# Six unread products in TensorE's pauses of the first attention batch, and a PSUM bank set aside for them

## The chip, the cores and the metric

The kernel runs on one core of a Trainium2 chip. The metric is the device time of one execution in microseconds (us). The core has TensorE (PE: matrix products, with PEld for its weight loads), VectorE (DVE), ScalarE (ACT), GpSimd (POOL) and SyncE (SP, whose queue issues every DMA here). TensorE's clock is granted by the chip at one of two levels, 2.4 GHz (written 1.00 in the profile) or 1.2 GHz (0.50).

## The reference

Three parts follow one another on 4 batches of 576 positions. First attention with 8 heads of 64: four heads look at the last 32 positions, four at positions of the same residue modulo 32. Then a maxout layer of width 768 and a PReLU layer of width 2048.

```python
scores = scale * np.matmul(q, k.transpose(0, 1, 3, 2))
scores = np.where(masks[None, :, :, :], scores, -1000000000.0)
attn = np.exp(scores - np.max(scores, axis=-1, keepdims=True))
attn = attn / (np.sum(attn, axis=-1, keepdims=True) + 1e-09)
x = np.matmul(attn, v)                                  # then laid out as (2304, 512)
x = np.maximum(np.maximum(x @ w1, x @ w2), x @ w3) @ w_out
h = x @ w_in
out = (np.maximum(h, 0.0) + alpha * np.minimum(h, 0.0)) @ w_out2
```

## The kernel before

The program has two halves. In the first (to about 396 us) attention and the maxout layer of the four batches are woven together; in the second (L959, L802) the PReLU layer runs over three blocks of 768 rows. The change touches the first half alone.

The weaving is done by the class `Weave`. Each piece of work is a task with an engine, a cost, a position and what it needs and gives. `plan` goes through them once, on the host, with these planned costs (in ns): it keeps the time at which each engine is free, picks the next task that can start, and writes down an order. `run` then emits every task in that order, so that the order on each engine is fixed in the program. Buffers are counted as rings: `place` lets a task that makes a buffer start only when the user of the buffer made so many places earlier is done. PSUM is one such ring, of eight banks of 512 columns, and nearly every task of PE takes one.

A unit of attention (`attention_tasks`) is two heads of one group of positions; a batch has eight units. On PE it runs `scores` (L314, a product in float32 of 64 rows, of which the trace shows two instructions), two `transposes` (L355) and `values` (L380). Between them stand DVE's masking with the row minimum (L322), ACT's exponential (L329), DVE's reciprocal (L340, L341), the normalising by DVE (L262) or ACT (L260), a copy of the transposes (L247, name pt) and the split of the result into a high and a low part (L247 and L250, name x). PE's order puts scores of one unit between transposes and values of others.

The products of the maxout layer (`gate_products`, L542, and `out1_products`, L564) are float32r products of 288 columns, twelve or eighteen to a task. Their weights come through SP's queue as words of a double (L425), are joined by ACT and DVE (L439, L443, L445) and split by ACT and DVE into a high and a low part (L247, L250, name w). From about 42 us on these products fill PE.

The constants (the identity and three masks) are made by POOL in `build_constants`, before everything else.

Of the kernel before, what the change touches and what calls it, by code (L numbers as in the profile page):

```python
# [10 lines left out]
F32 = mybir.dt.float32  # L11
# [7 lines left out]
DM = 512  # L19
F1 = 768  # L20
F2 = 2048
P = 128
# [6 lines left out]
QT = 96  # L29
KT = 128  # L30
# [14 lines left out]
class Weave:  # L45
# [11 lines left out]
    def __init__(self, rings):  # L57
        self.rings, self.made = dict(rings), {ring: [] for ring in rings}
        self.tasks, self.givers, self.users, self.banks = [], {}, {}, set()
        self.order = {ring: [] for ring in ("q", "v", "e", "pt", "x", "word")}  # L60

    def add(self, engines, emit, pos, needs=(), gives=(), makes=(), uses=(), mode=None, slack=0):
        t = len(self.tasks)
        if engines[0][0] != "PE" and any(key in self.banks for key in uses):
            pos -= self.URGENT
        self.banks.update(key for ring, key in makes if ring == "bank")
        self.tasks.append((engines, emit, pos, needs, makes, mode, slack))
        for ring, key in makes:
            if ring in self.order:
                self.order[ring].append(key)  # L70
        for e in gives:
            self.givers.setdefault(e, []).append(t)
        for key in [key for _, key in makes] + list(uses):
            self.users.setdefault(key, []).append(t)
# [19 lines left out]
    def plan(self, seed=None, near=120, change=100, slack=1.0, delay=350, shift=0.0):  # L94

        rng = random.Random(seed)
        sway = [rng.uniform(-shift, shift) if task[2] > -self.URGENT / 2 else 0.0 for task in self.tasks]
        delays = {"PE": 300, "ACT": delay, "DVE": delay, "SP": 2300}
        self.made = {ring: [] for ring in self.rings}
        free = dict.fromkeys(delays, 0)  # L100
        left = [sum(len(self.givers[e]) for e in task[3]) for task in self.tasks]
        at = [0] * len(self.tasks)
        ready = {t for t, n in enumerate(left) if not n}
        done, mode, order = {}, None, []
        while ready:
            options = {}
            for t in ready:
                engines, _, pos, _, makes, m, wait = self.tasks[t]
                when = self.place(makes, done)
                if when is None:  # L110
                    continue
                when = max(when, at[t] + slack * wait)
                best = None
                for e, cost in engines:
                    start = max(when, free[e])
                    if best is None or start + cost < best[0] + best[2]:
                        best = (start, e, cost)
                start, e, cost = best
                if m is not None:
                    start += change * (m != mode)  # L120
                options.setdefault(e, []).append(
                    (start, pos + sway[t] - (m is not None and m == mode), t, cost))
            pick = None
            for e, c in options.items():
                first = min(o[0] for o in c)
                o = min((o for o in c if o[0] <= first + near), key=lambda o: (o[1], o[0], o[2]))
                if pick is None or o[0] < pick[1][0]:
                    pick = (e, o)
            e, (start, _, t, cost) = pick
            makes, m = self.tasks[t][4:6]  # L130
            ready.remove(t)
            order.append((t, e))
            for ring, key in makes:
                self.made[ring].append(key)
            mode = mode if m is None else m
            free[e] = start + cost
            done[t] = start + cost + delays[e]
            for u in self.takers.get(t, ()):
                left[u] -= 1
                same = e == "PE" == self.tasks[u][0][0][0]  # L140
                at[u] = max(at[u], start + cost if same else done[t])
                if not left[u]:
                    ready.add(u)
        assert len(done) == len(self.tasks)
        return order

    def run(self, **settings):
        self.takers = {}
        for t, task in enumerate(self.tasks):
            for e in task[3]:  # L150
                for g in self.givers[e]:
                    self.takers.setdefault(g, []).append(t)
        for t, e in self.plan(**settings):
            self.tasks[t][1](e)


@with_exitstack
def attention_maxout_prelu_kernel(
# [13 lines left out]
    nc = tc.nc  # L172
    PSUM = bass.MemoryType.PSUM
    ctx.enter_context(tc.manual_schedule())

    const = ctx.enter_context(tc.tile_pool(name="const", bufs=1, side="left"))
    ident = const.tile([P, P], F32, name="ident")
    mask_l = const.tile([QT, KT], F32, name="mask_l")
    mask_l0 = const.tile([QT, KT], F32, name="mask_l0")
    mask_s = const.tile([P, 126], F32, name="mask_s")  # L180
    alpha_sb = const.tile([P, NF2], F32, name="alpha_sb")

    def build_constants():
        g = nc.gpsimd
        make_identity(nc, ident)
        for m in (mask_l0, mask_l):
            g.memset(m, 0.0)
            g.affine_select(out=m, in_=m, compare_op=ALU.is_ge, fill=BIG, base=32,
                            pattern=[[-1, KT]], channel_multiplier=1)
            g.affine_select(out=m, in_=m, compare_op=ALU.is_ge, fill=BIG, base=-1,  # L190
                            pattern=[[1, KT]], channel_multiplier=-1)
        g.affine_select(out=mask_l0, in_=mask_l0, compare_op=ALU.is_ge, fill=BIG, base=-32,
                        pattern=[[1, KT]], channel_multiplier=0)
        g.memset(mask_s, 0.0)
        ms = mask_s.rearrange("p (r a) -> p r a", a=NA)
        g.affine_select(out=ms, in_=ms, compare_op=ALU.is_ge, fill=BIG, base=0,
                        pattern=[[-NA, 7], [-1, NA]], channel_multiplier=1)
        g.affine_select(out=ms, in_=ms, compare_op=ALU.is_ge, fill=BIG, base=NA - 1,
                        pattern=[[NA, 7], [0, NA]], channel_multiplier=-1)
# [10 lines left out]
    hx, xx, x0x, ax, psx, conv_x = (ExitStack() for _ in range(6))  # L210

    def pool(stack, name, bufs, side="left"):
        return stack.enter_context(tc.tile_pool(name=name, bufs=bufs, side=side, reuse_waits="tile"))
# [19 lines left out]
    raw_p = pool(conv_x, "raw", 3, "right")  # L233
    words_p = pool(conv_x, "words", 8, "right")
    wst = pool(conv_x, "wst", 2, "right")
    ps = psx.enter_context(tc.tile_pool(name="ps", bufs=8, space=PSUM))

    def bank():
        return ps.tile([P, 512], F32, tag="bank", name="bank")


    weave = Weave({"bank": 8, "q": 2, "v": 2, "e": 3, "pt": 4, "x": 11, "t": 4, "h": 12,
                   "raw": 3, "word": 8, "wst": 2})
    add, tl = weave.add, {}

    def copy(e, out_, in_):
        (nc.scalar.copy if e == "ACT" else nc.vector.tensor_copy)(out_, in_)  # L247
# [478 lines left out]

    homes = [("gate", f, g) for f in range(NF1) for g in range(3)] + [("mix", f) for f in range(NF1)]
    build_constants()
    nc.sync.dma_start(alpha_sb, alpha)
    for b in range(B):  # L730
# [282 lines left out]
    for n in range(NQ * NBLK):  # L1013
        blk, q = divmod(n, NQ)
# [73 lines left out]
```

## Time and profile before

| | |
|---|---|
| median of 3 runs | 763.51 us (762.62 to 764.78) |
| profiled execution | 764.85 us, of which the span of instructions is 762.9 us |
| PE busy | 741.8 us, 97% of the span |
| DVE, ACT busy | 596.8 and 454.7 us (78% and 60%) |
| mean granted clock of TensorE | 0.991 |

The profile is one execution. Its span runs from the first to the last instruction; the 1.95 us between it and the execution's own time lie around it. A busy share is a mean over stages that differ much, so the stretches are looked at one by one.

### The profile page before, as it was taken

The numbers are of one execution on the slowest core, as the hardware profiler recorded it, in microseconds if no ns is written. First come the engines' busy times: TensorE is split into PE (matmuls) and PEld (weight loads), VectorE is DVE, ScalarE is ACT, GpSimd is POOL, SyncE is SP. The second block draws the span as 40 slices with busy tenths as digits, with TensorE's granted clock in tenths as the row PEclk, the third lists the DMA queues.
The fourth block names the chain that finished last, engine by engine and source line by source line (L and its number), as shares of the span: only waits on it lengthen the run. The fifth ranks groups of instructions, "written<-read, shape, count | busy, mean of one in ns | idle before, by whom it ended". The sixth has DMA issues, their size and how long they took to land.

```text
span 762.9 us, 16093 instructions
## 1 busy us (share of the span) xinstructions
PE 741.8 (97%) x5704; PEld 723.0 (95%) x5704; DVE 596.8 (78%) x1670; ACT 454.7 (60%) x1226; POOL 3.2 (0%) x16
## 2 busy tenths in 40 slices
PE   5899999999999999999999999999999999999997
PEld 4699999999999999999999999999999999999997
DVE  5999999888777987336368988878888877888894
ACT  6988897756665775323246566624666644566561
POOL 1000000000000000000000000000000000000000
PEclk9699999999999999999999999999999999999999
DMA  7387769877878856566938889999888999878361
GB/s 245 130 259 232 240 216 326 271 273 255 300 248 282 270 202 213 171 259 192 362 113 285 273 289 320 386 403 334 291 285 301 354 401 328 273 239 259 121 194 59
DMA packets 85471, 199.37 MB, mean 261 GB/s; under 512 B 10640, under 2 KB 40848, under 8 KB 85392
## 3 DMA queue, kind: packets, MB, share of 16 engines
q1 hardware_dynamic: 85392, 198.35, 75.9%
q8 instruction: 45, 0.74, 0.4%
q14 instruction: 34, 0.28, 0.1%
HBM read 148.51 MB, written 49.81 MB: 260 GB/s over the span
## 4 chain that ended last, share of the span: by engine, by line
PE 77%; DVE 12%; DMA 5%; ACT 2%; issue 2%; SPq 1%; DVEq 0%; ACTq 0%
PE bank L542 27%; PE ph L959 20%; PE po L802 15%; PE bank L564 9%; PE bank L314 3%; PE bank L380 2%; PE bank L355 2%; DVE g L796 2%; DVE c L806 2%; DMA w<-wh 1%; DMA w<-wp 1%; DVE e L322 1%; DMA xs<-x 1%; DMA x<-xd 1%; DVE c L964 1%
## 5 line engine op out<-in xcount | busy, mean ns | idle before, releaser
L542 PE MATMUL bank<-x,w 128*128 128x288 f32 x1728 | 236.5, 297 | 0.3 <-DVE t L553 0.3
L542 PEld LDWEIGHTS bank<-x,w 128*128 128x128 f32 x1728 | 231.1, 189 | 2.1 <-DVE t L553 0.6
L959 PE MATMUL ph<-x,w 128*128 128x384 f32 x1008 | 203.4, 337 | 1.8 <-DVE c L964 1.2
L802 PE MATMUL po<-w,g 128*128 128x256 f32 x1296 | 183.8, 282 | 1.7 <-DVE g L796 0.8
L802 PEld LDWEIGHTS po<-w,g 128*128 128x128 f32 x1296 | 175.4, 189 | 4.2 <-DVE g L796 3.2
L959 PEld LDWEIGHTS ph<-x,w 128*128 128x128 f32 x1008 | 168.3, 188 | 3.0 <-DVE c L964 1.9
L964 DVE TENSOR_TENSOR c<-ph,c 128x384 f32<-128x384 f32 x168 | 91.0, 554 | 32.7 <-PE ph L959 31.8
L795 ACT CAST g<-c 128x384 fp32r<-128x384 f32 x96 | 48.5, 505 | 89.7 <-DVE c L946 53.0
L564 PE MATMUL bank<-h,w 128*128 128x288 f32 x576 | 79.9, 297 | 0.4 <-DVE nm L322 0.4
L564 PEld LDWEIGHTS bank<-h,w 128*128 128x128 f32 x576 | 76.9, 188 | 1.8 <-DVE nm L322 0.8
L250 DVE TENSOR_TENSOR w<-word,w 128x512 fp32r<-128x512 f32 x88 | 55.4, 637 | 23.9 <-ACT w L247 23.5
L329 ACT ACTIVATE e<-e,nm 96x128 f32<-96x128 f32 (+2 forms) x176 | 68.0, 394 | 6.0 <-DVE nm L322 6.0
L916 ACT ACTIVATE c<-c 128x384 f32<-128x384 f32 x96 | 50.5, 526 | 33.9 <-DVE c L964 32.9
L247 ACT CAST w<-word 128x512 fp32r<-128x512 f32 x88 | 50.6, 582 | 32.0 <-DMA wh<-w 17.7
L917 ACT ACTIVATE c<-c,nalpha 128x384 f32<-128x384 f32 x96 | 59.2, 617 | 3.1
L920 DVE SCALAR_TENSOR_TENSOR c<-c 128x384 f32<-128x384 f32 x96 | 53.0, 552 | 9.0 <-ACT c L917 9.0
L796 DVE TENSOR_TENSOR g<-c,g 128x384 fp32r<-128x384 f32 x96 | 52.9, 551 | 1.9 <-ACT g L795 1.9
L796 DVE TENSOR_TENSOR g<-k,g 128x384 fp32r<-128x384 f32 x72 | 36.8, 550 | 14.4 <-ACT g L795 14.4
L439 ACT ACTIVATE word<-raw 128x512 f32<-128x512 f32 x56 | 37.4, 677 | 11.5 <-DMA raw<-in_w 5.9
L445 DVE SCALAR_TENSOR_TENSOR word<-raw,word 128x512 uint32<-128x512 uint32 x56 | 38.8, 693 | 1.9
L631 DVE TENSOR_TENSOR t<-bank,t 128x288 f32<-128x288 f32 x72 | 32.6, 452 | 7.8 <-PE bank L542 7.1
L795 ACT CAST g<-k 128x384 fp32r<-128x384 f32 x72 | 33.4, 515 | 7.8 <-PE po L802 4.4
(72 smaller groups left out, 679.8 us busy)
## 6 DMA issues: line engine op xcount, KB each, us to landing
w<-wh SPq DMA_DIRECT2D x72, 512.0 KB, 5.0
raw<-in_w SPq DMA_DIRECT2D x50, 512.0 KB, 4.5
w<-wo SPq DMA_DIRECT2D x48, 512.0 KB, 5.9
w<-wp SPq DMA_DIRECT2D x36, 512.0 KB, 6.3
wh<-w SPq DMA_DIRECT2D x24, 512.0 KB, 3.7
xd<-xst SPq DMA_DIRECT2D x28, 384.0 KB, 3.5
x<-xd SPq DMA_DIRECT2D x28, 384.0 KB, 8.1
wp<-w SPq DMA_DIRECT2D x24, 256.0 KB, 3.0
```

What stands on the lines that cost most here:

```text
L247: (nc.scalar.copy if e == "ACT" else nc.vector.tensor_copy)(out_, in_)
L250: nc.vector.tensor_tensor(out=out_, in0=x, in1=y, op=ALU.subtract)
L329: nc.scalar.activation(tl[ek][:nq, j, i, :nk], tl[ek][:nq, j, i, :nk], AF.Exp, bias=tl["nm", u][:nq, j, i:i + 1], scale=-1.0, accum_out=tl ...
L542: nc.tensor.matmul(acc, words["gate", f, g][:, wi, cc * P:(cc + 1) * P], xt[b, cc, hf][:, xi, :], start=n == 0, stop=n == 3 * NCC - 1)
L564: nc.tensor.matmul(acc, words["mix", f][:, wi, dc * P:(dc + 1) * P], st["h", hf, f][:, xi, :], start=n == 0, stop=n == 3 * NF1 - 1)
L795: nc.scalar.copy(g[:, 0], x)
L796: return g, lambda: nc.vector.tensor_tensor(out=g[:, 1], in0=x, in1=g[:, 0].bitcast(F32), op=ALU.subtract)
L802: nc.tensor.matmul(bank[:, NH * half:NH * (half + 1)], g[:, gi, t * P:(t + 1) * P], w[:, wi, off:off + NH], start=first and i == 0, stop=l ...
L917: nc.scalar.activation(a, a, AF.Copy, scale=nalpha[:, f:f + 1])
L920: nc.vector.scalar_tensor_tensor(out=a, in0=h, scalar=0.0, in1=a, op0=ALU.max, op1=ALU.add)
L959: nc.tensor.matmul(bank, words["h", n, i][:, wi, off + c * P:off + (c + 1) * P], x2h[blk, k, c][:, xi, :], start=m == 0, stop=m == 5)
L964: nc.vector.tensor_tensor(out=out_, in0=bank, in1=other, op=ALU.add)
```

## The change

Six products whose result nobody reads are put on PE in the first batch. Their operand is a tile `dense` of 96 x 128 float32 numbers, made by an `iota` on POOL ahead of the other constants (into the place of `mask_l0`, as integers) and a converting copy on DVE. One product has `dense` as its weights and the same tile, repeated four times, as its 512 moving columns. It writes a PSUM bank of its own, which is taken from the ring of the other tasks: that has seven banks now.

Where the planner finds a task of PE that starts more than 900 planned ns after PE is free (but not counting what lies before 1500 ns, and not from 46000 ns on), it puts products ahead of that task in the order: two ahead of PE's first task, and for every later pause its length over 1700, rounded down. They are not counted in the planner's own times.

```diff
@@ class Weave
+    FILL_FIRST, FILL_FROM, FILL_UNTIL, FILL_LEAST, FILL_COST = 2, 1500, 46000, 900, 850
@@ plan
             ready.remove(t)
+            idle = start - max(free[e], self.FILL_FROM)
+            if e == "PE" and start < self.FILL_UNTIL and idle > self.FILL_LEAST:
+                n = int(idle // (2 * self.FILL_COST)) if free[e] else self.FILL_FIRST
+                order.append((None, n))
             order.append((t, e))
@@ run
         for t, e in self.plan(**settings):
-            self.tasks[t][1](e)
+            if t is None:
+                self.fill(e)
+            else:
+                self.tasks[t][1](e)
@@ attention_maxout_prelu_kernel
+    dense = const.tile([QT, KT], F32, name="dense")
     def build_constants():
         g = nc.gpsimd
+        numbers = mask_l0.bitcast(mybir.dt.int32)
+        g.iota(numbers, pattern=[[7919, KT]], base=1234567, channel_multiplier=104729)
+        nc.vector.tensor_copy(dense, numbers)
         make_identity(nc, ident)
...
-    ps = psx.enter_context(tc.tile_pool(name="ps", bufs=8, space=PSUM))
+    ps = psx.enter_context(tc.tile_pool(name="ps", bufs=7, space=PSUM))
+    idle_ps = psx.enter_context(tc.tile_pool(name="idle_ps", bufs=1, space=PSUM))
...
-    weave = Weave({"bank": 8, "q": 2, "v": 2, "e": 3, "pt": 4, "x": 11, "t": 4, "h": 12,
+    weave = Weave({"bank": 7, "q": 2, "v": 2, "e": 3, "pt": 4, "x": 11, "t": 4, "h": 12,
                    "raw": 3, "word": 8, "wst": 2})
+    idle_bank = idle_ps.tile([P, 512], F32, name="idle_bank")
+    wide = dense[:, None, :].to_broadcast([QT, DM // P, P])
+    def fill(n):
+        for _ in range(n):
+            nc.tensor.matmul(idle_bank[:, :DM], dense, wide, start=True, stop=True)
+    weave.fill = fill
```

## Rows read from the trace of the kernel before

**Rows 1.** The page: engines' busy time, PE's clock in 40 slices, shares of the chain.

```profile
PE 741.8 (97%) x5704; PEld 723.0 (95%) x5704; DVE 596.8 (78%) x1670; ACT 454.7 (60%) x1226; POOL 3.2 (0%) x16
...
PEclk9699999999999999999999999999999999999999
...
PE 77%; DVE 12%; DMA 5%; ACT 2%; issue 2%; SPq 1%; DVEq 0%; ACTq 0%
```

**Rows 2.** Windows: stretch, its length, busy of PE, PEld, DVE, ACT, POOL, PEclk, DMA.

```profile
5.00:16.00 11.00, 7.93 (x60) 6.61 (x62) 7.57 (x59) 7.99 (x39) 0.00 (x0) 1.00 0.93 299
16.00:26.20 10.20, 6.77 (x84) 4.94 (x81) 8.78 (x61) 10.01 (x46) 0.00 (x0) 1.00 0.45 145
26.20:40.00 13.80, 12.73 (x89) 10.65 (x90) 12.01 (x57) 11.33 (x45) 0.00 (x0) 0.51 0.44 142
42.40:130.00 87.60, 87.11 (x749) 84.31 (x748) 85.15 (x283) 73.89 (x234) 0.00 (x0) 1.00 0.77 252
```

**Rows 3.** Waits of PE after 42.3 us: total, times, longest, the largest group.

```profile
PE ph L959 <- DVE c L964: 1.2, 3, 0.5
```

**Rows 4.** Groups by form, PE, 5 to 14 us: scores of the 108 form.

```profile
L314 PE MATMUL bank<-k,q 64*108 64x108 f32 x24 | 2.8, 403 | 6.1 <-DMA k<-in_kTs 6.1
```

**Rows 5.** The same view, 27 to 34 us.

```profile
L314 PE MATMUL bank<-k,q 64*108 64x108 f32 x12 | 1.4, 406 | 0.0
```

**Rows 6.** The same view, 40 to 42.3 us.

```profile
L314 PE MATMUL bank<-k,q 64*108 64x108 f32 x12 | 0.7, 254 | 0.0
```

**Rows 7.** Timeline of PE, 4 to 22 us: start, length, work, idle before.

```profile
5.02 2.30 PE L314 MATMUL bank<-k,q 64*108 64x108 f32 x20 [5.02 <-DMA k<-in_kTs]
8.37 1.42 PE L314 MATMUL bank<-k,q 64*108 64x108 f32 x12 [1.05 <-DMA k<-in_kTs]
11.79 1.30 PE L355 MATMUL bank<-ident,e 108*108 108x108 f32 x6 [2.00 <-DVE e L262]
...
19.65 0.67 PE L355 MATMUL bank<-ident,e 108*108 108x108 f32 x3 [1.48 <-DVE e L262]
20.25 0.90 PE L314 MATMUL bank<-k,q 64*96 64x128 f32 x12
```

**Rows 8.** Timeline of PE, 22 to 60 us.

```profile
26.47 0.72 PE L355 MATMUL bank<-ident,e 96*128 96x96 f32 x3 [2.22 <-DVE e L262]
...
34.34 1.49 PE L355 MATMUL bank<-ident,e 96*128 96x96 f32 x6 [0.80 <-ACT e L260]
35.53 3.23 PE L542 MATMUL bank<-x,w 128*128 128x288 f32 x12
...
39.85 0.72 PE L355 MATMUL bank<-ident,e 96*128 96x96 f32 x6
...
42.35 17.86 PE L542 MATMUL bank<-x,w 128*128 128x288 f32 x133
```

**Rows 9.** Waits of ACT, 6 to 43 us: total, times, longest.

```profile
ACT pt L247 <- PE bank L355: 1.7, 3, 0.7
ACT x L247 <- PE bank L380: 1.7, 4, 0.8
```

**Rows 10.** Waits of DVE, 6 to 43 us.

```profile
DVE e L322 <- PE bank L314: 9.9, 6, 6.6
DVE x L250 <- ACT x L247: 1.5, 3, 0.8
DVE pt L247 <- PE bank L355: 0.5, 1, 0.5
```

**Rows 11.** Timeline of all engines, 0 to 30 us: POOL's constants, DVE's first work.

```profile
0.74 0.20 POOL masks.py:197 MEMSET ident<- 128x128 f32 x1 [0.29 <-POOLq L1079]
...
3.92 0.33 POOL L198 TENSOR_SCALAR_AFFINE_SELECT mask_s<-mask_s 128x126 f32<-128x126 f32 x1
...
6.56 0.27 DVE L322 CUSTOM_DVE_ANT_0 e<-bank,mask_s 108x108 f32<-108x108 f32 x1 [6.56 <-PE bank L314]
```

**Rows 12.** Timeline of DVE, 26 to 50 us: the third weight's low part.

```profile
43.22 0.69 DVE L250 TENSOR_TENSOR w<-word,w 128x512 fp32r<-128x512 f32 x1
```

More of the change, by code (lines that the diff above doesn't have):

```diff
@@ L60, in __init__, with fill @@
         self.order = {ring: [] for ring in ("q", "v", "e", "pt", "x", "word")}
+    FILL_FIRST, FILL_FROM, FILL_UNTIL, FILL_LEAST, FILL_COST = 2, 1500, 46000, 900, 850
+    def fill(self, n):
+        raise NotImplementedError
     def add(self, engines, emit, pos, needs=(), gives=(), makes=(), uses=(), mode=None, slack=0):
```

## The prediction

> **What bounds the kernel now.** The page comes first: PE is busy 97% of the span and carries 77% of the chain that ended last; its clock stands at a full digit except in the second of 40 slices [rows 1]. The windows then show where that share holds. From 42.4 us PE is busy 87.11 of 87.60 us, while between 5 and 40 us it is not [rows 2], and after 42.3 us its largest group of waits is 1.2 us [rows 3]. So from 42 us on PE sets the pace, and what the start gains or loses is carried to the end, as long as DVE, at 85.15 of 87.60 us almost as full, comes forward with it.
>
> Next, the clock. The windows give 0.51 from 26.2 to 40 us and 1.00 before [rows 2]. The second figure can't be taken as read. The same scores (64x108) take 403 ns in the mean before 14 us [rows 4], 406 ns in the stretch marked 0.50 [rows 5], and 254 ns after 40 us [rows 6]. Until some time before 16 us TensorE therefore ran at 1.2 GHz too; the profile has no record of the clock there. In the timeline it is at 2.4 GHz by 20.25 us (twelve scores of 128 columns in 0.90 us) [rows 7], and low again from the transposes at 26.47 us, behind a pause of 2.22 us, through the first maxout products (twelve in 3.23 us, against 133 in 17.86 us from 42.35 us on, which is 1.61 for twelve) [rows 8].
>
> Last, whom the slow clock holds up. Between 6 and 43 us ACT waits for PE 1.7 and 1.7 us [rows 9], DVE 9.9 us of which 6.6 us is the start, then 1.5 us behind ACT and 0.5 us [rows 10]: 3.4 us of ACT, 5.3 of DVE. In between, from 16 to 26.2 us at the full clock, ACT is busy 10.01 of 10.20 us [rows 2]: there ACT sets the pace, not PE.
>
> **Where the six products go.** The planner's own starts (its planned ns, not times of the chip), followed through the tasks of before, have PE idle 2676 ahead of the first scores, 1574 ahead of the third scores, and 3015, 2160, 2190 and 1910 ahead of four transposes; all others up to 46000 are under 900. By the rule that is two, none, and four times one: six. The four places are those where the trace has PE waiting 2.00, 1.48, 2.22 and 0.80 us [rows 7, 8].
>
> **Price of one.** The trace has no such product. Of a float32 product it shows two instructions, so 1024 columns. Twelve scores of 128 columns in 0.90 us make 0.59 ns a column [rows 7], which gives 0.60 us; these use half the rows each and may overlap. Six transposes of 96 in 0.72 us make 1.25 ns [rows 8], which gives 1.28 us. I take 0.85 us, near the middle and what the diff counts with; at the low clock 1.7 us, between 1.2 and 2.56 us.
>
> **The two at the start.** POOL's first constant starts at 0.74 us; an iota between a memset (0.20) and a select (0.33), then a DVE copy like its 0.27 us row [rows 11], and the hand-overs, make `dense` ready at about 1.5 us (an estimate). Two at the low clock end at 1.5 + 3.4 = 4.9 us, just before the scores' operands at 5.02 us [rows 7]; by the bounds between 3.9 and 6.6, so 0 to 1.6 us late. I take 0. POOL's other constants move back by that third of a us, and the memset of `mask_l0` waits for DVE's copy; behind it in POOL's queue stand the masks, the last done at 3.92 + 0.33 = 4.25 us and first read at 6.56 [rows 11]. That cover is 2.3 us; without it every unit would start late by what is over. DVE has nothing before 6.56. No DMA is added or moved, and SP's queue stays as it is.
>
> **The four in pauses.** At the full clock 0.85 us fits into 2.00, 1.48 and 2.22 us, and is 0.05 us over in 0.80 us [rows 7, 8]: nothing, at most 0.48 us by the upper price.
>
> **What they may bring.** With PE at 2.4 GHz from the first scores to 42 us, PE alone would need about half of 7.93 and of 12.73 us [rows 2] less: 10 us. This is no forecast, since others hold the pace then. The third weight shows it: its low part is done at 43.22 + 0.69 = 43.91 us [rows 12], and its unit, the second after 42.35 [rows 8], starts at 42.35 + 1.61 = 43.96. PE can't come forward further than DVE and ACT do. ACT's idle time in 26.2 to 40 us is 13.80 - 11.33 = 2.47 us [rows 2], all inside the slow stretch; PE's work there shrinks by some 6 us, so I take 2.4 us as gone. Of ACT's 3.4 us of waits [rows 9] 0.9 us are left for the start; ACT can't begin earlier than its first scores, and when the clock rises between 5 and 16 us is open, so I take 0.6. Sum: 2.4 + 0.6 - 0 - 0 = 3.0 us. The far end is DVE's 5.3 us.
>
> **The seventh bank.** In the planner's record of before, three of 284 banks taken by the eighth place were still held by the task seven places back, by 34, 247 and 602 planned ns; the others had been free. So the order should stay nearly the same. Taken: 0; far end 0.9 us, if all three are waits on the chip.
>
> **Does one product hold the clock?** The clock fell behind the pause of 2.22 us, and not behind those of 2.00 and 1.48 us, of which the first is in the low stretch anyway [rows 7, 8]. In the stretch that followed PE was busy 12.73 of 13.80 us, and yet it stayed at 1.2 GHz until about 40 us [rows 2]. So it isn't shown that 0.85 us more in a pause is enough. The Trainium skill (TensorE: Matmul & The Clock Gate, Part 1, "What's actually happening") lets the clock follow how busy PE has recently been, by which any work in the pause would do. Its Part 4 (PE-mode transpose) says that transposes don't count as busy in the same way, which speaks against the change, because three of the four pauses lie between other work and transposes. By the first the sum stands at 3.0 us, by the second the clock may fall beside the products. The trace of the slow stretch leans to the second.
>
> **The rivals.** (1) My forecast: the clock rises with the first scores or soon after, and is held to 42 us. 3.0 us less. (2) It rises early and is not held behind 24 us: the 2.4 us fall away, 0.6 stays, with up to 0.5 more or less: 762.4 to 763.4. For it: the busy stretch that stayed low. (3) The clock is held, but DVE's weights don't come forward, because they wait for loads or for other DVE work: DVE is full from 42 us [rows 2] and the third weight has no slack [rows 12]; 763.0 or so. Against it: DVE has 5.3 us of waits to give before that. (4) Slower: the clock stays low and the products are in the way of PE's next task. At 1.7 us each they are over by 0.22 and 0.90 us: 1.1 us, 764.6. At 2.56 us it is 1.6 + 0.56 + 1.08 + 0.34 + 1.76 = 5.3 us, 768.8. It counts as slower from a price of about 2.0 us on (0.5 + 0.5 + 1.2 = 2.2). Against it: two dense products in a row are more work for PE than anything else before 16 us. (5) The bank ring makes another order or waits: 763.5 to 764.4, more if the order turns out worse all through.
>
> **How the numbers follow.** The sum against the profiled execution is 764.85 - 3.0 = 761.85 us; that execution lies 1.34 us above the median shown, so the forecast is 763.51 - 3.0 = 760.5 us. Faster or slower counts from 0.3% on, 2.3 us, about what a measurement of this kernel can tell from no change. Chances: (1) 0.55, with 758.6 to 761.6 as its own range (0.50 faster, 0.05 same); (2) 0.18 (0.02 faster, 0.16 same); (3) 0.12 same; (4) 0.10 (0.07 slower, 0.03 same); (5) 0.05 (0.03 same, 0.02 slower). Together 0.52 faster, 0.39 same, 0.09 slower. The range goes from DVE's 5.3 us less, 758.2, to rival 4 at its taken price, 764.6.
>
> **What the profile will show.** Right: the 64x108 scores near 254 ns from 8 us on, PEclk 1.00 from 26 to 40 us, the dense run of maxout products starting near 39.4 instead of 42.35 us, and ACT's and DVE's waits for PE before 43 us mostly gone. Six products of two instructions at the named places, each 0.6 to 1.28 us. Wrong: PEclk 0.5 again behind 24 us (2), PE waiting for w or t after 40 us (3), products of 2 us and transposes starting later behind them (4), PE waiting for a bank's reader (5).

## The result: 0.74% slower, where 0.4% faster was forecast

Over 12 runs each the changed kernel takes 771.94 us in the median (766.11 to 774.44), the kernel before 765.54 us (762.62 to 769.39). The ratio is 1.0074, 95% interval 1.0050 to 1.0098, some 5.7 us. The forecast was 760.5 us with a range up to 764.6 us; it took off from the 763.51 us of three runs. The profiled execution of the changed kernel has a span of 772.5 us; at 774.32 us it is one of the slowest of the twelve.

The page of the changed kernel: busy time of the engines, and PE's clock in 40 slices.

```profile
PE 754.3 (98%) x5718; PEld 727.4 (94%) x5718; DVE 600.4 (78%) x1680; ACT 453.0 (59%) x1217; POOL 3.4 (0%) x17
...
PEclk9899999999999999999999999999999999999999
```

PE has 14 instructions more than in [rows 1], so seven products and not six; most of its 12.5 us of longer busy time are these (10.9 us), and they lie in what were pauses. Its windows, in the stretches of [rows 2]:

```profile
5.00:16.00 11.00, 10.40 (x65) 7.33 (x64) 7.76 (x59) 8.28 (x40) 0.00 (x0) 1.00 0.90 306
26.20:40.00 13.80, 12.92 (x115) 10.03 (x115) 12.99 (x67) 12.80 (x55) 0.00 (x0) 0.75 0.37 130
42.40:130.00 87.60, 83.23 (x689) 79.51 (x689) 80.91 (x263) 68.54 (x214) 0.00 (x0) 0.98 0.73 245
```

Behind 26.2 us the clock is at 0.75 in the mean where it was 0.51, and ACT is busy 12.80 us instead of 11.33: that much went as meant. The loss is in the last row. From 42.4 to 130 us PE is busy 83.23 us, not 87.11. The timeline of PE, 0 to 62 us, to be held against [rows 7, 8]:

```profile
1.38 3.78 PE L270 MATMUL idle_bank<-dense 96*128 96x512 f32 x4 [1.38 <-DVE dense L202]
5.12 2.30 PE L342 MATMUL bank<-k,q 64*108 64x108 f32 x20
...
24.64 1.05 PE L270 MATMUL idle_bank<-dense 96*128 96x512 f32 x2
27.08 0.69 PE L383 MATMUL bank<-ident,e 96*128 96x96 f32 x3 [1.39 <-DVE e L290]
...
33.55 1.88 PE L270 MATMUL idle_bank<-dense 96*128 96x512 f32 x2
35.27 0.81 PE L383 MATMUL bank<-ident,e 96*128 96x96 f32 x6
...
40.80 1.12 PE L270 MATMUL idle_bank<-dense 96*128 96x512 f32 x2
41.36 2.54 PE L570 MATMUL bank<-x,w 128*128 128x288 f32 x14
44.46 17.76 PE L570 MATMUL bank<-x,w 128*128 128x288 f32 x132 [0.57 <-DVE w L278]
```

Behind the two products the scores start at 5.12 us, 0.1 us later than before; a product takes 1.8 to 1.9 us at the low clock and, where it stands alone, 1.04 to 1.12 us at the high one. The 20 scores behind them take 2.30 us, as before: the clock did not rise. The groups by form, 5 to 14 us, say the same (403 ns in [rows 4], 254 ns at 2.4 GHz in [rows 6]):

```profile
L342 PE MATMUL bank<-k,q 64*108 64x108 f32 x24 | 2.8, 403 | 0.6 <-DMA k<-in_kTs 0.6
```

By 41.36 us PE is 1.0 us ahead of the kernel before, and a seventh product, which the other order brought, stands in front of that. Then it waits. Waits of PE from 42.3 to 420 us (total, times, longest), where the kernel before has 2.2 us in all, the longest 0.7 us:

```profile
PE bank L383 <- DVE x L278: 1.7, 1, 1.7
PE bank L570 <- DVE x L278: 1.5, 1, 1.5
PE bank L570 <- ACT pt L275: 1.5, 1, 1.5
PE bank L570 <- DVE t L581: 1.0, 1, 1.0
PE bank L383 <- DVE t L659: 0.9, 1, 0.9
PE bank L342 <- ACT pt L275: 0.6, 1, 0.6
PE bank L570 <- DVE w L278: 0.6, 1, 0.6
```

With one more of 0.2 us these are 8.0 us, 5.8 more. Two of the places are followed by a stretch at the low clock (windows behind the waits at 125.7 and at 283.6 us; the last figures are PEclk, DMA share and GB/s):

```profile
127.00:130.50 3.50, 3.50 (x25) 3.22 (x25) 3.36 (x11) 3.15 (x13) 0.00 (x0) 0.54 0.59 228
284.00:287.60 3.60, 3.60 (x19) 3.60 (x18) 3.52 (x10) 2.97 (x13) 0.00 (x0) 0.54 1.03 306
```

In each some 3.4 us run at half speed, which costs about 1.7 us. 5.8 + 3.4 = 9.2 us. To be explained are the difference of the two spans, 772.5 - 762.9 = 9.6 us, and the 1.0 us by which PE led at 41.36 us, so some 1.4 us stay open. In this execution the loss lies behind 42 us, in PE waiting for readers of its banks and in the falls of the clock behind two such waits, and not in the products. How much of the 5.7 us between the kernels such falls make isn't shown: over the twelve runs the mean granted clock is 0.994, no lower than over the 35 runs of the kernel before that were made beside e1.

### The profile page after: what moved, and what is told of

The parts are those of the page before. It is cut to its first block, busy times and chain, and to the rows that moved or that the text cites. A ratio compares the mean times of both kernels' runs of the same rounds, so it can differ in the third digit from the quotient of the medians.

```text
span 772.5 us, 16118 instructions
## 1 busy us (share of the span) xinstructions
PE 754.3 (98%) x5718; PEld 727.4 (94%) x5718; DVE 600.4 (78%) x1680; ACT 453.0 (59%) x1217; POOL 3.4 (0%) x17
## 4 chain that ended last, share of the span: by engine, by line
PE 68%; DVE 15%; DMA 9%; ACT 4%; issue 3%; SPq 1%; DVEq 0%; ACTq 0%
PE ph L987 20%; PE bank L570 18%; PE po L830 15%; PE bank L592 9%; DMA wp<-w 2%; DMA raw<-in_w 2%; PE bank L342 2%; DVE g L824 2%; PE bank L408 2%; DVE c L834 2%; PE bank L383 2%; DVE e L350 1%; DMA w<-wh 1%; DVE w L278 1%; DVE word L473 1%
```

## The experiments

All times are ratios to the kernel before, run on the same chip, with a 95% interval.

| kernel | products | banks in ring, in pool | ratio |
|---|---|---|---|
| the change | 7 | 7, 7 | 1.0074 (1.0050 to 1.0098) |
| e1_ring7 | none | 7, 7 | 1.0085 (1.0060 to 1.0111) |
| e3_order7 | none | 7, 8 | 1.0019 (0.9995 to 1.0044) |
| e4_pool7 | none | 8, 7 | 1.0026 (0.9997 to 1.0054) |
| e5_ring7_near125 | none | 7, 7, another order | 1.0098 (1.0061 to 1.0134) |
| e9_fill_order8_pool7 | 6 | 8, 7 | 1.0030 (1.0011 to 1.0049) |
| e11_change_late8 | 7 | 7, 7 and 8 behind the weave | 1.0055 (1.0036 to 1.0075) |
| e12_change_pool8 | 7 | 7, 8 | 1.0031 (1.0005 to 1.0056) |
| e2_fill8 | 6 | 8, 8 | 0.9978 (0.9959 to 0.9998) |
| e6_first8 | the first 2 | 8, 8 | 1.0007 (0.9987 to 1.0026) |
| e7_pauses8 | the 4 in pauses | 8, 8 | 1.0006 (0.9984 to 1.0027) |
| e10_three_first8 | 3 and 4 | 8, 8 | 0.9974 (0.9956 to 0.9993) |
| e8_first8of8 | 8 ahead of the first scores | 8, 8 | one run, 771.71 us |
| l0_light | none, lighter DVE and ACT | 8, 8 | 0.9972 (0.9950 to 0.9994) |
| l1_light_fill | 6, lighter DVE and ACT | 8, 8 | 0.9953 (0.9929 to 0.9977) |

**The bank or the products?** Four kernels take the change apart. e1 (lines shortened):

```diff
-    ps = ... bufs=8 ...          weave = Weave({"bank": 8, ...
+    ps = ... bufs=7 ...          weave = Weave({"bank": 7, ...
```

> The kernel before with seven banks in the planner's ring and seven in the pool, and no products. Theory A (the order that the planner writes for seven banks costs the time): about 0.7 to 1.0% slower than before, 5 to 8 us, with PE pauses over 1 us near 88, 126, 283 and 347 us as in the changed kernel. Theory B (the products stand in the way of PE's own tasks): within 0.3% of before.

e2, the products alone, with ring and pool at eight (shortened):

```diff
     def bank():
-        return ps.tile([P, 512], F32, tag="bank", name="bank")
+        t = ps.tile([P, 512], F32, tag="bank", name="bank")
+        for _ in range(due_fill.pop() if due_fill else 0):
+            nc.tensor.matmul(t[:, :DM], dense, wide, start=True, stop=True)
+        return t
...
     def fill(n):
+        if n:
+            due_fill.append(n)
```

> The changed kernel with eight banks in ring and pool; the products are written into the bank that PE's next task is about to take, so no bank is set aside and the order stays that of before. Theory A: within 0.5% of before, on either side, and no pauses over 1 us after 60 us. Theory B: 0.5 to 1.0% slower than before. The forecast of the record, if only the bank was what failed: 3 us faster.

e3 has 7 in the ring alone, e4 in the pool alone.

> Ring of seven in the planner alone, eight banks in the pool, no products: the other order without the scarcer bank. Theory A: as slow as the kernel with seven of both, 5 to 8 us. Theory C (PE waits on the chip for a bank to be read): within 0.3% of before.

> Order of before (ring of eight in the planner), seven banks in the pool, no products. Theory A: within 0.3% of before, at most 0.9 us for the three banks that the planner's record has still held. Theory C: 5 to 8 us slower, with PE waiting for readers of a bank.

e1 loses as much as the change without one product, and e2 gains 0.22% (1.7 us): theory B is out. Theories A and C, as they were put, both fall: the order alone and the pool alone cost 0.2 to 0.3% each, neither clear of nothing by its interval, and both together 0.85%. That both cost more than the sum of the two isn't clear of the noise either. The waits of PE in e1, 42.3 to 420 us, show what comes on top:

```profile
PE bank L542 <- DVE t L553: 2.1, 1, 2.1
PE bank L314 <- DMA k<-in_kTl: 1.5, 1, 1.5
PE bank L542 <- DVE x L250: 1.1, 1, 1.1
PE bank L355 <- DVE x L250: 1.1, 1, 1.1
```

The wait for k comes with this order, with eight banks too (e3 has 1.9 us of it); in the changed kernel's own profile PE waits 1.5 us for ACT's pt just ahead of these scores, at 88 us, and then not for k. The wait of 2.1 us for t is gone in e3, and its place is best seen in e4, which has the order of before. Timeline of e4, 325 to 345 us:

```profile
335.31 0.56 DVE L677 TENSOR_TENSOR t<-xs 128x384 f32<-128x384 f32 x1 [10.21 <-DMA xs<-x]
...
338.03 1.01 DVE L553 TENSOR_TENSOR t<-bank,t 128x288 f32<-128x288 f32 x2
...
338.54 6.74 PE L542 MATMUL bank<-x,w 128*128 128x288 f32 x37 [2.20 <-DVE t L553]
```

The same stretch of the kernel before:

```profile
334.50 0.56 DVE L677 TENSOR_TENSOR t<-xs 128x384 f32<-128x384 f32 x1 [9.92 <-DMA xs<-x]
...
337.22 1.01 DVE L553 TENSOR_TENSOR t<-bank,t 128x288 f32<-128x288 f32 x2
...
337.72 7.44 PE L542 MATMUL bank<-x,w 128*128 128x288 f32 x54 [0.32 <-DVE t L553]
```

This is behind the weave, where no planner orders anything. DVE waits 10 us for a load, and the readers of PE's banks stand in its queue behind that wait. PE goes on into free banks, a unit of 1.6 us (twelve products) into each. With eight it runs out 0.32 us before DVE comes back, with seven 2.20 us. How long DVE waits differs from execution to execution (8.95 to 11.23 us), so PE's pause alone tells little. What stays the same is the difference of the two waits: it is 9.60 or 9.61 us in all eight profiles with eight banks in which PE pauses here (among them 10.57 less 0.97 us in e2 and 11.23 less 1.63 us in e7), and 8.01 or 8.02 us in all five with seven. With eight banks PE bridges 9.6 us, with seven 8.0 us: one bank is one unit of 1.6 us. In the changed kernel's own profile DVE waits only 8.97 us, which eight banks would have bridged. Timeline of the changed kernel, 332 to 348 us:

```profile
343.45 0.56 DVE L705 TENSOR_TENSOR t<-xs 128x384 f32<-128x384 f32 x1 [8.97 <-DMA xs<-x]
...
346.68 1.49 PE L570 MATMUL bank<-x,w 128*128 128x288 f32 x9 [0.96 <-DVE t L581]
```

**Is the order for seven an accident?** The planner is greedy, and its own end for PE moves by some planned us with any of its parameters. With near at 125 it is as short for seven banks as it was for eight.

```diff
-    weave.run()
+    weave.run(near=125)          # seven banks in ring and pool, no products
```

> Seven banks in ring and pool, no products, but the planner's parameter near at 125 in place of 120, with which its own end for PE is 312.1 planned us for seven banks (with 120 it is 317.4 for seven and 312.5 for eight). Theory A (the order written for seven banks costs the time, and that order is an accident of a greedy planner): within 0.4% of before. Theory C (seven banks as such cost it): 0.6 to 1.1% slower, as with the order of near 120.

1.0098, over six runs: theory A falls here too. A plan as short as that for eight banks doesn't help, and a second order for seven banks loses as much on the chip as the first.

**The eighth bank given back in parts.** e9 is the change with the planner's ring left at 8.

> The changed kernel with the planner's ring left at eight: products and a bank set aside, seven banks in the pool, the order of before. If order and pool cost only together (0.2% and 0.3% alone, 0.85% both): within 0.3% of before, so 0.5 to 1% faster than the change as made. If the bank as such costs the time: 0.6% or more slower.

1.0030, at the edge of the first case; its interval ends below the second. e11 is the change, but `bank()` takes every eighth bank from `idle_ps` once the weave has run. e12 is e2 with the planner's ring at 7.

> The changed kernel as made (order for seven, seven banks in the weave), but behind the weave the set-aside bank joins the rotation of the maxout products, so that PE can run eight units ahead of DVE there. Theory G (a part of the loss is the pause of about 2 us near 336 to 346 us, where DVE waits 10 us for a load and PE runs out of banks one unit of 1.6 us earlier): 1.3 to 2 us faster than the changed kernel, that is 0.5 to 0.6% slower than before, and the pause at most 0.4 us. Rival (the pause there is DVE's or the load's, whatever the banks): as the changed kernel, 0.7 to 0.9% slower.

> The changed kernel with its order (planner's ring of seven) and its products, but eight banks in the pool and none set aside; the products go into the bank of PE's next task. If the scarcer pool under that order is what costs: 0.2% slower than before to 0.2% faster (0.19% for the order alone, less 0.2% for the products). If the products cost time in this order: 0.6% or more slower.

The trace bears theory G out: no wait for the maxima of that stage is left in e11, where DVE waits 9.11 us. The ratio falls from 1.0074 to 1.0055, as the theory had it, but the intervals overlap, so the times alone don't show it. What remains in e11 beside the wait for k is the 1.5 us behind DVE's x (a product that waits until DVE has read attention values out of a bank), with a stretch at 0.52 of the clock behind it. Waits of PE, 42.3 to 420 us, and the window behind that wait:

```profile
PE bank L348 <- DMA k<-in_kTl: 1.5, 1, 1.5
PE bank L576 <- DVE x L284: 1.5, 1, 1.5
```

```profile
282.00:285.40 3.40, 3.40 (x16) 3.31 (x14) 3.31 (x10) 2.46 (x10) 0.00 (x0) 0.52 1.00 271
```

With eight banks throughout (e12) this one goes too, and the wait for k stays: 1.0031. By the ratios, some 0.2 of the 0.74% is the stretch behind the weave, some 0.2 waits for banks inside it, and 0.3 the order, with the products in. Each of these steps is smaller than the intervals of the two ratios that it lies between, so the split is an estimate; their sum is not in doubt.

**What do the products do?** Halves of e2:

```diff
-                n = int(idle // (2 * self.FILL_COST)) if free[e] else self.FILL_FIRST
+                n = 0 if free[e] else self.FILL_FIRST                        # e6
+                n = int(idle // (2 * self.FILL_COST)) if free[e] else 0      # e7
+                n = 0 if free[e] else 8                                      # e8
```

> Eight banks, order of before, and only the two products ahead of the first scores. If the gain of all six with eight banks (0.2%) comes from an early rise of the clock: 1 to 2 us faster than before. If these two do nothing, as the 108 column scores at 1.2 GHz behind them in the changed kernel say: within 0.15% of before.

> Eight banks, order of before, and only the four products in the pauses. If these make the gain, by a shorter stretch at 1.2 GHz behind 26 us: 1 to 2 us faster than before. If the gain is that of the first two: within 0.15%.

> One look with eight banks and eight products ahead of the first scores, none in the pauses: does the clock rise from these products before 16 us at all? If it follows dense work of PE within some us, the first products take 1.8 us each and the last 0.85 to 0.95 us, and the scores start at about 11 us. If these products don't raise it, all eight take 1.8 us, the scores start near 16 us, and the kernel is 8 to 11 us slower.

Neither half moves the time, 1.0007 and 1.0006; the two don't add up to the 0.9978 of all six, and their intervals are too wide to say more. What eight products in a row do is clear. Groups by form, 0 to 12 us, of e8:

```profile
L259 PE MATMUL bank<-dense 96*128 96x512 f32 x16 | 9.0, 729 | 1.4 <-DVE dense L202 1.4
L345 PE MATMUL bank<-k,q 64*108 64x108 f32 x24 | 1.6, 262 | 0.0
```

Eight take 9.0 us, not 14: the clock rose among them, and the scores behind them run at 262 ns. So such products do raise it in this execution, while the two of the changed kernel, followed by scores, did not. Behind the 3.10 us wait that follows these scores it fell again: scores of 126 columns take 273 ns ahead of that wait and 456 ns behind it. The next kernel has three:

```diff
-    FILL_FIRST, ... = 2, ...
+    FILL_FIRST, ... = 3, ...     # e2 otherwise
```

> Six products with eight banks and a third one ahead of the first scores (seven in all). Eight of them in a row raised the clock at 5.0 us, during the third. If three do: 64x108 scores at 254 ns from 6 us on, and 0.2 to 0.5% faster than before. If the clock falls again in the wait for the second k, or doesn't rise: 0.1 to 0.3% slower than with two, within 0.2% of before.

Timeline of PE in e10, 0 to 44 and 115 to 124 us:

```profile
1.38 4.87 PE L259 MATMUL bank<-dense 96*128 96x512 f32 x6 [1.38 <-DVE dense L202]
6.18 1.28 PE L345 MATMUL bank<-k,q 64*108 64x108 f32 x20
...
13.26 1.10 PE L386 MATMUL bank<-ident,e 126*126 126x126 f32 x4
...
20.45 0.65 PE L386 MATMUL bank<-ident,e 126*126 126x126 f32 x4
...
38.24 5.93 PE L573 MATMUL bank<-x,w 128*128 128x288 f32 x40
...
119.64 1.00 PE L345 MATMUL bank<-k,q 64*126 64x126 f32 x8 [0.59 <-ACT pt L278]
```

The scores start 1.16 us later than before and take 1.28 instead of 2.30 us. From about 12 to 15.5 us this execution is at 1.2 GHz again (the same four transposes take 1.10 us at 13.26 us and 0.65 us at 20.45 us; PEclk is 0.50 from 13 to 15 us), then at 2.4 GHz, and its dense run starts at 38.24 us, 4.1 us ahead of [rows 8]. At 0.9974 (2 us) it has the lowest ratio of the kernels that compute the reference; from e2 (0.9978) it can't be told apart.

Is it the third product that raised the clock? e12 begins with two, as the changed kernel does. Timeline of PE in e12, 0 to 17 us:

```profile
5.14 1.78 PE L345 MATMUL bank<-k,q 64*108 64x108 f32 x20
8.42 0.82 PE L345 MATMUL bank<-k,q 64*108 64x108 f32 x12 [1.50 <-DMA k<-in_kTs]
```

Here the clock rose during the first scores, behind two products. So it did in e9 (1.83 and 0.82 us), and in l1 (below) before the second scores (2.30 and 0.82 us); in the change, e2, e6 and e11, with the same two products, both stay slow (2.30 and 1.42 us), as in all seven profiles without a product there. One execution each can't tell three products from two.

**Where does the lead go?** In e10 it is 4.1 us at 38 us, but the scores of 119.64 us stand at 121.48 us in the kernel before: 1.84 us are left. In e7, same order again, the clock is 1.00 from 26 to 39 us, and the lead goes from 3.35 to 0.49 us. PE in e7, the window and the timeline:

```profile
26.20:39.00 12.80, 12.12 (x127) 8.98 (x127) 12.59 (x65) 12.80 (x51) 0.00 (x0) 1.00 0.51 167
```

```profile
39.00 7.29 PE L573 MATMUL bank<-x,w 128*128 128x288 f32 x50
...
120.99 1.00 PE L345 MATMUL bank<-k,q 64*126 64x126 f32 x8 [0.59 <-ACT pt L278]
```

ACT is busy 12.80 of 12.80 us there: with the clock held, ACT is the pace. In e10, task by task against the kernel before, 0.55 us of the lead goes in the dense run up to 69 us, 0.9 us among the attention products of 93 to 99 us and 0.8 us at the transposes and scores of 117 to 120 us, with PEclk at 1.00 from 42.4 to 130 us in both. To tell whether DVE and ACT take the lead back, both were made lighter, without products (l0) and with them (l1). These two leave out part of the work on the maxout weights: ACT's rebasing and DVE's low part; the products read the high part alone (cuts marked).

```diff
-            rebase_words(tl[rk], tl[ak])
+            if not light: rebase_words(tl[rk], tl[ak])
...
-            lambda _: sub(tl[tk][:, 1, :n], ...)
+            lambda _: light or sub(tl[tk][:, 1, :n], ...)
...
-    words["gate", f, g][:, wi, ...]
+    words["gate", f, g][:, 0, ...]
```

> The kernel before with less work for DVE and ACT between 20 and 100 us: for the 24 weight tiles that stay (maxout layer) ACT's rebasing and DVE's low part are left out, the words are joined from shifted raw words, and the maxout products read the high part alone; instructions on PE, SP and their order stay. Its output is no longer the reference's. It is the base for the next kernel; PE should run ahead of the kernel before by 1 to 4 us at 125 us.

> The same lightened kernel with the six products and eight banks. Theory D (the 1 to 3 us that the products bring by 40 us are given back to DVE and ACT between 40 and 125 us, because these are full there): with these two relieved the lead is kept, 2 to 3 us (0.25 to 0.4%) ahead of the lightened kernel without products, and at 125 us in the profile at least two thirds of the lead at 40 us. Theory F (it is lost to chance falls of the clock later on, whatever DVE and ACT do): no more than the 0.2% of six products with eight banks, and the lead steps down where PEclk falls.

PE in l0, timeline of 36 to 60 and 117 to 125 us, and the window of [rows 2]:

```profile
41.29 18.94 PE L547 MATMUL bank<-x,w 128*128 128x288 f32 x141
...
120.35 1.00 PE L314 MATMUL bank<-k,q 64*126 64x126 f32 x8 [0.38 <-ACT pt L247]
```

```profile
42.40:130.00 87.60, 87.22 (x750) 84.42 (x749) 73.06 (x254) 62.74 (x210) 0.00 (x0) 1.00 0.77 256
```

The timeline of l1, 34 to 60 and 115 to 123 us:

```profile
38.92 21.28 PE L578 MATMUL bank<-x,w 128*128 128x288 f32 x159
...
117.95 1.00 PE L345 MATMUL bank<-k,q 64*126 64x126 f32 x8 [0.39 <-ACT pt L278]
```

With DVE at 73 instead of 85 us of 87.6, l1 leads l0 by 2.37 us at 39 us and by 2.40 us at 118 us: nothing is given back. The kept lead is what theory D asked of the profile, in these two executions; theory F asked for a lead that steps down where the clock falls, and that of e10 went without a fall. The times don't decide: l1 is 0.19% (1.7 us) ahead of l0, less than theory D's 0.25 to 0.4% and within theory F's 0.2%, and inside the intervals.

## Why the prediction was wrong

**The step that failed** is "The seventh bank": "Taken: 0; far end 0.9 us". It measured 0.85%, 6.5 us (e1). The reasoning had three holes. It counted in the planner's record how many banks were still held, and concluded that the order would stay; but the order changed (a seventh product is put in, and 24 scores stand at 91.53 us, where before 12 stood at 96.35 us and 24 at 100.60 us), and it brought waits of its own (for k near 90 us in e1, e3, e11 and e12). It took the record for the chip: on the chip readers are later than planned, and PE waits for banks that the plan had free (1.5 us behind DVE's x). And it looked only at the weave. Behind it the pool's depth is what PE runs on while DVE waits 10 us for a load; [rows 3] sums the waits of before to almost nothing, and does not tell that PE already ran out of banks there, by 0.32 us, so that nothing was left to give. Rival 5 was the right one, at a chance of 0.05 and with 763.5 to 764.4 us; only its last words, "more if the order turns out worse all through", reach what was measured.

**What bounds the kernel**: right on the clock, which was low before 16 us without a record of it, and right for losses: PE's waits behind 42 us show in the time. e8, whose scores start 5.3 us late, was 5.8 us over the median of the kernel before, in its one run (of which a mean clock of 0.989 may be a part). For gains it was right only in part, as shown below.

**Where the products go**: six places right; the seventh came from the other order. **Price of one** and **the two at the start**: near enough, 1.8 to 1.9 us at the low clock against 1.7 taken and 1.04 to 1.12 us at the high one against 0.85 (within the bounds stated), and 0.1 us late. **The four in pauses**: right for two. Those at 9.37 and 33.55 us began at the low clock, took 2.07 and 1.88 us and ran up to the transposes behind them, which may be late by some tenths of a us; for the first, the sum used the price at the full clock in a pause that the prediction itself places in the low stretch.

**What they may bring**: right in mechanism up to 42 us, where the clock was held. The lead there is 1.0 us in the change as made, 0.9 us in e2, 3.35 us in e7 and 4.1 us in e10, against 3.0 forecast. (The far end of 5.3 us counts 1.5 us in which DVE waited for ACT as if PE had caused them.) Wrong in "carried to the end": half or more of it is given back between 42 and 125 us, in the stretch where DVE is full. That is near to rival 3, given 0.12, and its condition stood in the prediction ("as long as DVE [...] comes forward with it"); what PE waits for in e10, though, are hand-overs of attention (DVE's t, ACT's pt) more than weights. With eight banks the products are worth 1.7 us by the ratio of e2; its interval, 0.2 to 3.1 us, just takes in the 3.0.

**Does one product hold the clock?** In the pauses it helps, it seems, but doesn't make sure of it. From 26.2 to 40 us the clock is 0.51 to 0.88 in the eight profiles without a product in the pauses (0.51 before, 0.88 in e1, e3 and l0), 0.75 in the change, e2 and e11, and 1.00 in e7, e9, e10, e12 and l1. In the change it fell behind a pause of 1.39 us that a product of 1.05 us had opened, and in e10 it fell at about 12 us behind a pause with a product in it. These are single executions, so it is likely and not proved. At the start, two products raised the clock in some executions and not in others. The Trainium skill (TensorE: Matmul & The Clock Gate, Part 1, "What's actually happening") lets the clock rise with PE's activity. The run of eight products agrees with it; the changed kernel does not as far as busy time goes, since PE was busy from 1.38 to 7.4 us and the scores at 8.02 us still ran at 1.2 GHz (1.42 us for twelve, 0.82 us in e12 behind a like start). The prediction left this question open, and it stays open.

**Rival 4**, slower by the products' own length, is out: e2, with its six products, is not slower.

## What to carry to other kernels

A buffer that looks unused in the mean may be the one that bridges the longest wait of its reader: before taking a bank out of a ring, look for the place where its reader is away longest, and count how many units the producer runs ahead there (here eight banks bridged a wait of 9.6 us, seven one of 8.0 us). A greedy planner's order was not stable under a small change of its rings, so a change and the re-planning that it causes are timed apart. And a lead that an engine wins at the start was kept where the engines that feed it were free to come forward, and for the most part given back where they were full; the windows of the kernel before showed where that was.

## What was not expected of the hardware

The clock's falls are not tied to this change. In e6, which has the order of before, it fell behind a pause of 1.24 us near 215 us (0.53 from 217.1 to 220.5 us), where the profiled kernel before had no fall. In e4 and e9 it fell behind the pauses of 2.20 and 2.00 us near 340 us, but in e1 not behind one of 2.05 us there. Such a fall costs 1.7 us, and the executions of one kernel spread over 4 to 10 us here. In the profiles of kernels of the same order the falls behind 42 us lie at a few places: the attention products near 125 us (e7) and 215 us (e6), and the hand-over near 340 us. Why some executions have these falls and others not stays open; a single profile per kernel can't tell it.
